# One core, attention and two MLP blocks: batch 2 alone through the first MLP, side-by-side heads, early conversions shared with GpSimd

## The chip, the cores and the metric

One core of a Trainium2 chip runs the whole program. The metric is the device time of one execution in microseconds; a smaller number is better. The kernel before has a median of 1398.46 us over 3 runs (1396.95 to 1399.26).

## The reference, cut to what matters

Four batches of 448 tokens and 768 channels pass through attention with capped scores, a layer norm with an MLP, and a mixer block with a token MLP and a second MLP. All of it is float32.

```python
# attention: batch 4, 12 heads, 448 tokens, 64 channels a head
scores = cap * np.tanh(np.matmul(q, k.transpose(0, 1, 3, 2)) * scale / cap)
attn = np.exp(scores - np.max(scores, axis=-1, keepdims=True))
attn = attn / (np.sum(attn, axis=-1, keepdims=True) + 1e-09)
x = np.matmul(attn, v)                       # to (4, 448, 768)
# first block
xn = (x - mu) / np.sqrt(var + 1e-06) * g_ln
x = x + np.maximum(xn @ w_ch1, 0.0) @ w_ch2  # 768 -> 3072 -> 768
# second block
h = np.maximum(x.transpose(0, 2, 1) @ w_tok1, 0.0) @ w_tok2   # 448 -> 256 -> 448
u = x + h.transpose(0, 2, 1)
out = u + np.maximum(u @ w_ch1, 0.0) @ w_ch2  # 768 -> 1536 -> 768
```

## The kernel before, in words

**Products.** Each float32 factor of the MLPs is split into a high and a low value in a rounded format that TensorE takes fast (`fp32r`), and a product is made of three matmuls: high by high, low by high, high by low (`PASSES`). Every matmul streams the 448 tokens of one batch.

**MLP.** The hidden channels are cut into groups of 512: six groups for the first MLP (0 to 5), three for the second (6 to 8). A group is four tiles of the first weight matrix (18 matmuls a batch each, line 587) and six tiles of the second (12 matmuls a batch each, line 608), so 144 matmuls for one batch. The results are taken out of PSUM by ScalarE and VectorE (lines 592, 593) and added to `x` by VectorE (line 612). `mlp(plan)` walks a list of (group, batches): with two batches ("a pair") one loaded weight tile serves both, with one batch ("alone") it serves one. Weight tiles lie in a ring of three (`split0` to `split2`).

**Weights.** When a tile is needed for the first time, `piece` loads the raw float32 words and converts them: two steps on ScalarE (lines 276, 277), three on VectorE (278, 279 and the addition in 280), a copy that gives the high value on either engine, and a subtraction that gives the low value on VectorE (recorded at line 172, the helper `low`). There are 14 pieces a group, 8 of 384 columns and 6 of 512. The result is also written to a buffer in HBM (`kept`, line 300), and every later use loads it from there (line 296).

**Heads.** Batches 0 and 1 do attention at the start of the program, in plain float32. The heads of batches 2 and 3 are woven into the MLPs of batches 0 and 1: one head at a time, 8 score matmuls (line 366), tanh and exp on ScalarE, a maximum on VectorE (line 374), high and low parts of the exponentials (`eh`, `el`), and the products with the values. These come in two forms. In the plain form (batch 2 before) high and low values go through 11 matmuls in three shapes (lines 411, 413, 414), and a column of ones gives the row sums (read by VectorE at line 433). With a batch in `BESIDE` (batch 3 before) high and low values stand side by side in one 128 column weight, 7 matmuls do (line 408), VectorE sums the exponentials itself (line 421) and the two halves are added (line 430). Lines 341 and 342 load a head's queries and keys (480 KB) and values (192 KB); a late head has one buffer for each, so each load waits for the head before. Two subtractions of a late head may go to GpSimd (also recorded at line 172).

**Order.** Every operation is a step with a key. `Program.emit` plays the steps through a list of costs and puts on each engine the ready step with the smallest key, so the order in the program is fixed when it is built. The numbers `T_...`, `PACE...`, `N...` set the keys. All loads of the late stages, all writes of `kept` and of the output stand in one queue, SyncE's (SP), and are issued in order.

**Sequence of the main stages.** Group 0 of batch 0 alone; groups 1 to 5 of the pair (0, 1); tokens of batch 0 woven with group 0 of batch 1; tokens of batch 1 woven with group 6 of batch 0; groups 7 and 8 of the pair; group 6 of batch 1 alone; then batch 2 alone for `n1` groups, the pair (2, 3) for the other groups of the first MLP, tokens of batch 2 woven with batch 3's `n1` groups alone, tokens of batch 3 woven with groups 6 and 7 of batch 2, the pair for group 8, and groups 6 and 7 of batch 3 alone.

Of the kernel before, what the change touches and what calls it, by code (L numbers as in the profile page):

```python
# [15 lines left out]
ALU = mybir.AluOpType  # L16
# [42 lines left out]

URGENT, SCORES, PREPARE, LOAD = 1000.0, 19.31, 4.58, 24.58  # L60

BESIDE = (3,)

N0, N1, N20, N2 = 1, 3, 1, 2
T_LN0, T_LN1 = 7.69, -20.0
T_AHEAD, N_AHEAD, AHEAD_PACE = 14.0, 1, 5.0
T_ALONE, STRETCH0, T_PAIR, STRETCH1 = 85.0, 1.3, 165.0, 1.14
T_ATT2, PACE2, T_ATT3, PACE3 = 171.18, 25.0, 500.0, 40.0
LEAD, RAW_AHEAD, EVACUATE, TOKENS_AHEAD = 6.3, 9.57, -7.49, 17.25


# [15 lines left out]
class Program:  # L87
# [11 lines left out]
    def add(self, engine, cols, run, reads=(), writes=(), early=0.0):  # L99

        names = [(name.strip("*+"), "*" in name, "+" in name) for name in engine.split("/")]
        costs = {e: self.FIXED[e] + self.RATE[e] * cols * (0.5 if half else 1.0) for e, half, _ in names}
        step = Step(costs, run, (self.key - early, len(self.steps)))
        step.port = {e for e, _, port in names if port}
        before = set()
        for b in [p for b in reads for p in b.parts]:
            before.add(b.writer)
            b.readers.append(step)  # L110
        for b in [p for b in writes for p in b.parts]:
            before.add(b.writer)
            before.update(b.readers)
            b.writer, b.readers = step, []
        before -= {None, step}
        for s in before:
            s.users.append(step)
        step.waits = len(before)
        self.steps.append(step)
# [32 lines left out]
def block_kernel(ctx: ExitStack, tc: tile.TileContext, qkv, cap, gln, w1, w2, wt1, wt2, con, out):  # L152
    nc = tc.nc
    mm, act, dve = nc.tensor.matmul, nc.scalar.activation, nc.vector
    engine_of = {"dve": nc.vector, "pool": nc.gpsimd}
    prog = Program()
    add = prog.add
# [13 lines left out]
    def low(eng, out, whole, high):  # L171
        eng.tensor_tensor(out, whole, high.bitcast(F32), op=ALU.subtract)  # L172

    def copy(e, out, a):
        if e == "act":
            act(out, a, AF.Copy)  # L176
        else:
            dve.tensor_copy(out, a)
# [20 lines left out]
    BIG = [[Box(t[:, e]) for e in range(NCC)] for t in big_t]  # L199
# [6 lines left out]
    def area(n):  # L206
        ends.append(ends[-1] + n)
        return area_t[:, ends[-2]:ends[-1]]
# [6 lines left out]
    two = [Box(area(S)), Box(area(S))]  # L215
# [17 lines left out]
    def ring(of):  # L233
        while True:
            yield from of
# [28 lines left out]


    raws, wholes = ring(RAW), ring(WHOLE)
    kept = {}

    def piece(src, m, target, to):

        r, w = next(raws), next(wholes)
        f = w.at.bitcast(I32)[:, :m]
        words = r.at.bitcast(I32)[:, :2 * m].rearrange("p (n two) -> p n two", two=2)
        lo, hi = words[:, :, 0], words[:, :, 1]
        add("dma", m, lambda: nc.sync.dma_start(out=r.at.bitcast(I64)[:, :m], in_=src), (), [r], early=RAW_AHEAD)
        add("act", m, lambda: act(f.bitcast(F32), hi.bitcast(F32), AF.Copy, scale=2.0 ** -112), [r], [w])  # L276
        add("act", m, lambda: act(lo, lo.bitcast(U32), AF.Copy, scale=2.0 ** -29), (), [r])  # L277
        add("dve+", m // 2, lambda: dve.tensor_scalar(f, f, 3, None, op0=ALU.logical_shift_left), (), [w])  # L278
        add("dve+", m, lambda: dve.scalar_tensor_tensor(f, hi, -(1 << 31), f, op0=ALU.bitwise_and, op1=ALU.bitwise_or), [r], [w])  # L279
        add("dve+", m, lambda: dve.tensor_tensor(f, f, lo, op=ALU.add), [r], [w])  # L280
        g = f.bitcast(F32)
        add("act/dve*+", m, lambda e: copy(e, target[:, 0], g), [w], to)
        add("dve+", m, lambda e: low(engine_of[e], target[:, 1], g, target[:, 0]), [w], to)

    def load(no, w, row, cols):

# [42 lines left out]
    def attention(b, start, pace):  # L329
        x = x_t[b]  # L330
        early, beside = b < 2, b in BESIDE
        rs, rm = rs_t[b % 2], rm_t[b % 2]
# [146 lines left out]
    centred = two + own  # L479
# [54 lines left out]
    def normalise(b):  # L534
        rstd = RSTD[0]
        eng = LN_ENGINES[b]
        for e in range(NCC):
            o, g = centred[e], BIG[b % 2][e]
            if b >= 2:
                subtract(b, e, o)  # L540
            add("dve+", S, lambda o=o, e=e: dve.scalar_tensor_tensor(
                o.at, o.at, gl[:, e:e + 1], rstd.at, op0=ALU.mult, op1=ALU.mult), [rstd, GL], [o])
            add("act", S, lambda g=g, o=o: act(g.at[:, 0], o.at, AF.Copy), [o], [g])  # L543
            add(eng, S, lambda eng, g=g, o=o: low(engine_of[eng], g.at[:, 1], o.at, g.at[:, 0]), [o], [g])
# [13 lines left out]
    def prepare(g):  # L558

        nonlocal n_tile  # L560
        rows = [(w1, g * G + i, C) for i in range(G)] + [(w2, g * NCC + e, G * P) for e in range(NCC)]
        for w, row, cols in rows:
            load(n_tile, w, row, cols)
            n_tile += 1
            prog.key += AHEAD_PACE
# [148 lines left out]
    with tc.manual_schedule():  # L714
        setup()
        prog.key = T_AHEAD
        for g in range(N_AHEAD):
            prepare(g)
        prog.key = 0.0
        attention(0, 0.0, 3.97)  # L720
        prog.key += T_LN0
        layer_norm(0)
        normalise(0)
        head_banks = side_banks = ring(BANKS[:2])
        attention(1, 60.01, 6.39)
        prog.key += T_LN1
        layer_norm(1)
        normalise(1)
        head_banks = side_banks = ring(BANKS[:1])

        main_banks = ring(BANKS[2:])
        n0, n1, n2 = N0, N1, N2
        prog.key, stretch = T_ALONE, STRETCH0
        weave(mlp(groups((0,), 0, n0)))
        main_banks = chain(BANKS[2:], ring(BANKS[1:]))
        attention(2, T_ATT2, PACE2)
        layer_norm(2)
        attention(3, T_ATT3, PACE3)
        prog.key, stretch = T_PAIR, STRETCH1
        weave(mlp(groups((0, 1), n0, NG1 - n0)))  # L740
        weave(tokens(0, HIDDEN[2]), mlp(groups((1,), 0, n0)), ahead=TOKENS_AHEAD)
        weave(tokens(1, HIDDEN[2]), mlp(groups((0,), NG1, N20)), ahead=TOKENS_AHEAD)
        weave(mlp(groups((0, 1), NG1 + N20, NG2 - N20), (0,)))
        weave(mlp(groups((1,), NG1, N20), (1,)))
        normalise(2)
        stretch = 1.0
        weave(mlp(groups((2,), 0, n1)))
        layer_norm(3)
        normalise(3)
        weave(mlp(groups((2, 3), n1, NG1 - n1)))  # L750
        weave(tokens(2, HIDDEN[2]), mlp(groups((3,), 0, n1)), ahead=TOKENS_AHEAD)
        weave(tokens(3, HIDDEN[2]), mlp(groups((2,), NG1, n2)), ahead=TOKENS_AHEAD)
        weave(mlp(groups((2, 3), NG1 + n2, NG2 - n2), (2,)))
        weave(mlp(groups((3,), NG1, n2), (3,)))
        prog.emit()
# [41 lines left out]
```

## Time and profile before

| | |
|---|---|
| median of 3 runs | 1398.46 us (1396.95 to 1399.26) |
| the profiled execution | 1399.07 us |
| its span, first to last instruction | 1397.3 us |
| TensorE busy (matmuls) | 1370.9 us, 98% |
| TensorE weight loads | 1178.4 us, 84% |
| VectorE busy | 887.7 us, 64% |
| ScalarE busy | 612.0 us, 44% |
| GpSimd busy | 63.2 us, 5% |
| moved by DMA | 262.16 MB, mean 188 GB/s |

The busy shares are means over stages of different kinds: VectorE is nearly full in the first 800 us, where weights are converted and heads run, and nearly idle after that. Matmuls overlap in the records (one is shown as some 365 ns long while the next starts some 203 ns after it), so the time that a matmul costs is read from start to start.

### The profile page before, as it was taken

How to read it: one execution, taken by the hardware profiler on the slowest of the kernel's cores; microseconds unless marked ns; L12 is line 12 of the kernel's file. 1: busy time of each engine (PE TensorE's matmuls, PEld its weight loads, DVE VectorE, ACT ScalarE, POOL GpSimd, SP SyncE). 2: the span in 40 equal slices, each digit the busy share in tenths (PEclk: the TensorE clock that was granted, in tenths of full speed). 3: DMA queues.
4: the chain of work that ended last, by engine and by line, in shares of the span. 5: the costliest groups of instructions: out<-in, count | busy, mean ns of one | idle time of the engine just before them, and what ended most of it. 6: DMA issues, size and time to landing. Idle time of an engine off the chain costs nothing.

```text
span 1397.3 us, 17773 instructions
## 1 busy us (share of the span) xinstructions
PE 1370.9 (98%) x6512; PEld 1178.4 (84%) x6512; DVE 887.7 (64%) x1602; ACT 612.0 (44%) x995; POOL 63.2 (5%) x52
## 2 busy tenths in 40 slices
PE   8999989999999999999999999999999999999998
PEld 3335578889898999988999999999999999999997
DVE  5999698988898899999989973212122232232221
ACT  7986567675657656776656421010100111111000
POOL 0000002010011001100010000000000000000000
PEclk9999999999999999999999999999999999999999
DMA  8885447667675756467565576643232456554366
GB/s 264 275 268 161 142 123 244 226 203 227 196 229 191 240 177 223 156 218 235 192 202 195 178 232 200 208 149 128 84 122 93 148 166 189 186 168 151 124 197 194
DMA packets 135671, 262.16 MB, mean 188 GB/s; under 512 B 10144, under 2 KB 72864, under 8 KB 135584
## 3 DMA queue, kind: packets, MB, share of 16 engines
q1 hardware_dynamic: 135008, 260.74, 57.9%
q8 instruction: 51, 0.84, 0.2%
q10 hardware_dynamic: 576, 0.29, 0.1%
q14 instruction: 36, 0.29, 0.1%
HBM read 198.86 MB, written 62.13 MB: 187 GB/s over the span
## 4 chain that ended last, share of the span: by engine, by line
PE 89%; DVE 6%; ACT 3%; DMA 1%; issue 1%; SPq 0%; ACTq 0%; DVEq 0%
PE bank L587 37%; PE bank L608 37%; PE sc L366 3%; PE bank L384 3%; PE bank L682 2%; PE bank L663 2%; PE bank L408 1%; PE sc L363 1%; DVE m L374 1%; ACT x L369 1%; PE bank L414 1%; PE bank L413 1%; PE bank L466 1%; ACT x L370 1%; PE bank L639 1%
## 5 line engine op out<-in xcount | busy, mean ns | idle before, releaser
L608 PE MATMUL bank<-h,split 128*128 128x448 f32 x2592 | 547.9, 367 | 3.4 <-DVE x L612 2.9
L587 PE MATMUL bank<-big,split 128*128 128x448 f32 x2592 | 548.1, 368 | 3.0 <-ACT big L543 2.0
L587 PEld LDWEIGHTS bank<-big,split 128*128 128x128 f32 x2592 | 485.9, 188 | 48.2 <-ACT big L543 3.3
L608 PEld LDWEIGHTS bank<-h,split 128*128 128x128 f32 x2592 | 484.9, 188 | 46.7 <-DVE x L612 3.6
L592 ACT ACTIVATE h<-bank 128x448 fp32r<-128x448 f32 x144 | 78.3, 544 | 398.1 <-PE bank L587 397.6
L612 DVE TENSOR_TENSOR x<-x,bank 128x448 f32<-128x448 f32 x216 | 133.4, 619 | 186.1 <-PE bank L608 184.0
L593 DVE SCALAR_TENSOR_TENSOR h<-bank,h 128x448 fp32r<-128x448 f32 x144 | 89.3, 621 | 183.9 <-ACT h L592 183.3
L276 ACT ACTIVATE whole<-raw 128x384 f32<-128x384 f32 (+2 forms) x130 | 77.6, 600 | 45.4 <-DVE split L172 42.0
L280 DVE CUSTOM_DVE_ANT_0 whole<-raw,whole 128x768 uint16<-128x768 uint16 (+2 forms) x130 | 85.6, 659 | 0.6
L172 DVE TENSOR_TENSOR split<-whole,split 128x384 fp32r<-128x384 f32 (+1 forms) x126 | 79.2, 632 | 4.3 <-ACT split L176 3.6
L279 DVE SCALAR_TENSOR_TENSOR whole<-raw,whole 128x384 int32<-128x384 int32 (+2 forms) x130 | 81.3, 627 | 0.2
L277 ACT ACTIVATE raw<-raw 128x384 int32<-128x384 uint32 (+2 forms) x130 | 77.6, 600 | 0.0
L176 ACT ACTIVATE split<-whole 128x384 fp32r<-128x384 f32 (+1 forms) x85 | 47.9, 564 | 43.6 <-PE bank L608 19.7
L172 POOL TENSOR_TENSOR ks<-area,ks 64x512 fp32r<-64x512 f32 x23 | 31.7, 1377 | 675.5 <-ACT ks L347 675.5
L374 DVE TRANSPOSE_TENSOR_REDUCE m<-x 128x28 f32<-128x896 f32 x48 | 52.5, 1101 | 8.2 <-ACT x L370 7.7
L278 DVE TENSOR_SCALAR whole<-whole 128x384 int32<-128x384 int32 (+2 forms) x130 | 53.7, 416 | 2.3 <-ACT whole L276 1.9
L374 DVE TRANSPOSE_TENSOR_REDUCE m<-area 128x28 f32<-128x896 f32 x48 | 52.9, 1102 | 0.8 <-ACT area L370 0.8
L369 ACT ACTIVATE area<-sc,tsc 128x896 f32<-128x896 f32 x48 | 48.2, 1005 | 11.1 <-DVE el L400 6.3
L370 ACT ACTIVATE area<-area,cap_t 128x896 f32<-128x896 f32 x48 | 49.9, 1040 | 0.6
L369 ACT ACTIVATE x<-sc,tsc 128x896 f32<-128x896 f32 x48 | 46.7, 996 | 6.9 <-DVE tsc L252 4.3
L394 ACT ACTIVATE eh<-area 128x896 fp32r<-128x896 f32 x48 | 45.4, 946 | 9.4 <-PE bank L408 3.5
L370 ACT ACTIVATE x<-x,cap_t 128x896 f32<-128x896 f32 x48 | 49.0, 1037 | 0.3
(117 smaller groups left out, 1116.0 us busy)
## 6 DMA issues: line engine op xcount, KB each, us to landing
split<-kept SPq DMA_DIRECT2D x136, 384.0 KB, 4.1
split<-kept SPq DMA_DIRECT2D x102, 512.0 KB, 3.7
raw<-in_w SPq DMA_DIRECT2D x72, 384.0 KB, 3.5
kept<-split SPq DMA_DIRECT2D x72, 384.0 KB, 3.6
raw<-in_w SPq DMA_DIRECT2D x54, 512.0 KB, 4.0
kept<-split SPq DMA_DIRECT2D x54, 512.0 KB, 3.3
area<-in_qkv SPq DMA_DIRECT2D x38, 480.0 KB, 4.1
area<-in_qkv SPq DMA_DIRECT2D x35, 192.0 KB, 3.3
```

The costliest lines, as they stand in the source:

```text
L172: eng.tensor_tensor(out, whole, high.bitcast(F32), op=ALU.subtract)
L276: add("act", m, lambda: act(f.bitcast(F32), hi.bitcast(F32), AF.Copy, scale=2.0 ** -112), [r], [w])
L279: add("dve+", m, lambda: dve.scalar_tensor_tensor(f, hi, -(1 << 31), f, op0=ALU.bitwise_and, op1=ALU.bitwise_or), [r], [w])
L280: add("dve+", m, lambda: dve.tensor_tensor(f, f, lo, op=ALU.add), [r], [w])
L369: add("act", 2 * S, lambda e=e, sc=sc: act(e, sc.at[:, :, :S], AF.Tanh, scale=tsc), [sc], eb)
L370: add("act", 2 * S, lambda e=e: act(e, e, AF.Exp, scale=cap_t), (), eb)
L374: add("dve", 2 * S, lambda half=half, e=e: dve.tensor_reduce(m.at[:, half].rearrange("p c j -> p (c j)"), e.rearrange("p c (j i) -> p (c j ...
L587: mm(ph.at[:, :S], w[:, wi, cc * P:(cc + 1) * P], src[cc].at[:, xi], start=(cc, n) == (0, 0), stop=(cc, n) == (NCC - 1, 2))
L592: add("act", S, lambda ht=ht, ph=ph: act(ht.at[:, 0], ph.at[:, :S], AF.Relu), [ph], [ht], early=EVACUATE)
L593: add("dve", S, lambda ht=ht, ph=ph: dve.scalar_tensor_tensor(ht.at[:, 1], ph.at[:, :S], 0.0, ht.at[:, 0].bitcast(F32), op0=ALU.max, op1=A ...
L608: mm(py.at[:, :S], w[:, wi, i * P:(i + 1) * P], h[i].at[:, hi], start=(i, n) == (0, 0), stop=(i, n) == (G - 1, 2))
L612: add("dve", S, lambda x=x, py=py: dve.tensor_tensor(x.at, x.at, py.at[:, :S], op=ALU.add), [py], [x], early=EVACUATE)
```

## The change

`BESIDE` takes batch 2 in, so both late batches use the side-by-side form. `N1` goes from 3 to 6: batch 2 does all six groups of the first MLP alone, no group is done by the pair (2, 3), and batch 3 does six groups alone. The late heads get other start keys and paces. In the group that is prepared ahead, at the start of the program, the integer addition (line 280) and the subtraction for the low value go to GpSimd. `normalise` for batches 2 and 3 uses two buffers in turn instead of six, so that it no longer shares the buffers of the late heads' exponentials.

```diff
-BESIDE = (3,)
+BESIDE = (2, 3)
-N0, N1, N20, N2 = 1, 3, 1, 2
+N0, N1, N20, N2 = 1, 6, 1, 2
-T_ATT2, PACE2, T_ATT3, PACE3 = 171.18, 25.0, 500.0, 40.0
+T_ATT2, PACE2, T_ATT3, PACE3 = 230.0, 35.0, 650.0, 25.0
-    kept = {}
+    kept, ahead = {}, False
@@ piece
-        add("dve+", m, lambda: dve.tensor_tensor(f, f, lo, op=ALU.add), [r], [w])
+        add("pool+" if ahead else "dve+", m, lambda e: engine_of[e].tensor_tensor(f, f, lo, op=ALU.add), [r], [w])
-        add("dve+", m, lambda e: low(engine_of[e], target[:, 1], g, target[:, 0]), [w], to)
+        add("pool+" if ahead else "dve+", m, lambda e: low(engine_of[e], target[:, 1], g, target[:, 0]), [w], to)
@@ normalise
-            o, g = centred[e], BIG[b % 2][e]
+            o, g = centred[e] if b < 2 else two[e % 2], BIG[b % 2][e]
@@ block_kernel
         prog.key = T_AHEAD
+        ahead = True
         for g in range(N_AHEAD):
             prepare(g)
+        ahead = False
```

On TensorE, this is the first head of batch 2 before, the first half of its products with the values among the MLP of the pair (0, 1):

```order
L587 MATMUL bank_112<-big_84,split_77 128x448 x12
L411 MATMUL bank_111<-eh_98,vs_97 96x448
L413 MATMUL bank_111<-eh_98,vs_97 64x448
L414 MATMUL bank_111<-el_99,vs_97 96x448
L411 MATMUL bank_111<-eh_98,vs_97 96x448
L413 MATMUL bank_111<-eh_98,vs_97 64x448
L414 MATMUL bank_111<-el_99,vs_97 96x448
L587 MATMUL bank_112<-big_84,split_77 128x448 x6
```

The same half head in the changed program:

```order
L587 MATMUL bank_114<-big_85,split_79 128x448 x12
L408 MATMUL bank_111<-eh_98,vs_97 128x448
L408 MATMUL bank_111<-el_99,vs_97 128x448
L408 MATMUL bank_111<-eh_98,vs_97 128x448
L408 MATMUL bank_111<-el_99,vs_97 128x448
L587 MATMUL bank_114<-big_85,split_79 128x448 x6
```

Six matmuls became four, and the half head stands some tiles later in the MLP. On VectorE, the first piece of the group prepared ahead stands so before (`whole` holds the words in work, `split` the result, `m` and `rs` belong to heads):

```order
L278 TENSOR_SCALAR whole_75<-whole_75 128x384
L279 SCALAR_TENSOR_TENSOR whole_75<-raw_72,whole_75 128x384
L280 ISA whole_75<-raw_72,whole_75 128x768
L374 TENSOR_REDUCE m_100<-x_82 128x28
L433 TENSOR_REDUCE rs_103<-bank_112 32x14
L172 TENSOR_TENSOR split_77<-whole_75,split_77 128x384
L278 TENSOR_SCALAR whole_76<-whole_76 128x384
```

and GpSimd does in the changed program, with the additions and subtractions gone from VectorE's row:

```order
L280 TENSOR_TENSOR whole_75<-whole_75,raw_72 128x384
L172 TENSOR_TENSOR split_77<-whole_75,split_77 128x384
L280 TENSOR_TENSOR whole_76<-whole_76,raw_73 128x384
L172 TENSOR_TENSOR split_77<-whole_76,split_77 128x384
L280 TENSOR_TENSOR whole_75<-whole_75,raw_74 128x384
```

In all 28 instructions move so, for 14 pieces. On SP's queue, where group 6 of batch 1 alone loads its tiles from `kept`, heads of batch 3 now load between them; before, these rows were the `kept` loads one after the other:

```order
L296 DMA split_79<-kept_27_0_219 128x2x384
L296 DMA split_79<-kept_27_384_220 128x2x384
L342 DMA area<-in_qkv 128x384
L296 DMA split_77<-kept_36_0_221 128x2x512
L296 DMA split_78<-kept_37_0_222 128x2x512
L341 DMA area<-in_qkv 128x960
L296 DMA split_79<-kept_38_0_223 128x2x512
```

After the last raw weight load of the program the queue held two loads of values before; it now holds six loads of values and four of queries and keys.

## Rows read from the trace of the kernel before

**Rows 1.** The chain that ended last, share of the span by engine (the page, 4).

```profile
PE 89%; DVE 6%; ACT 3%; DMA 1%; issue 1%; SPq 0%; ACTq 0%; DVEq 0%
```

**Rows 2.** Busy time of each engine in stretches of the span (the first row names columns).

```profile
core 0: us, PE busy (x) PEld busy (x) DVE busy (x) ACT busy (x) POOL busy (x), PEclk, DMA share, GB/s
205.00:550.00 345.00, 345.00 (x1685) 308.51 (x1684) 309.57 (x563) 225.94 (x375) 39.51 (x28) 1.00 0.66 214
550.00:600.00 50.00, 50.00 (x262) 46.60 (x261) 47.85 (x81) 40.11 (x66) 7.85 (x6) 1.00 0.57 188
600.00:650.00 50.00, 45.55 (x229) 41.02 (x228) 46.17 (x89) 32.75 (x63) 4.96 (x4) 0.97 0.71 233
```

**Rows 3.** Timeline of TensorE, one head of batch 2: start us, duration us, instruction.

```profile
275.32 0.36 PE L411 MATMUL bank<-eh,vs 128*96 128x448 f32 x1
...
276.55 0.99 PE L366 MATMUL sc<-qs,ks 128*128 128x448 f32 x4
...
281.09 0.36 PE L411 MATMUL bank<-eh,vs 128*96 128x448 f32 x1
...
282.41 0.97 PE L366 MATMUL sc<-qs,ks 128*128 128x448 f32 x4
```

**Rows 4.** Timeline of TensorE, a second and a first half head of batch 3.

```profile
709.74 0.36 PE L408 MATMUL bank<-eh,vs 128*128 128x448 f32 x1
...
710.35 6.35 PE L608 MATMUL bank<-h,split 128*128 128x448 f32 x30
...
718.61 0.37 PE L408 MATMUL bank<-eh,vs 128*128 128x448 f32 x1
...
719.43 8.67 PE L608 MATMUL bank<-h,split 128*128 128x448 f32 x42
```

**Rows 5.** Groups by line and shape, whole span: count, busy us, mean ns, idle before.

```profile
L172 POOL TENSOR_TENSOR qs<-area,qs 128x448 fp32r<-128x448 f32 x23 | 30.9, 1342 | 8.3 <-DVE qs L178 4.6 <-ACT qs L176 2.1
...
L421 DVE TRANSPOSE_TENSOR_REDUCE n<-area 128x28 f32<-128x896 f32 x24 | 26.3, 1097 | 0.0
...
L433 DVE TRANSPOSE_TENSOR_REDUCE rs<-bank 32x14 f32<-32x448 f32 x36 | 23.3, 648 | 17.0 <-ACT x L436 9.2 <-PE bank L414 3.8 <-PE sc L363 2.1
...
L430 DVE TENSOR_TENSOR x<-bank,area 64x448 f32<-64x448 f32 x12 | 7.3, 612 | 1.3 <-ACT area L429 1.1
```

**Rows 6.** The two conversion steps that move, all pieces (the page, 5).

```profile
L280 DVE CUSTOM_DVE_ANT_0 whole<-raw,whole 128x768 uint16<-128x768 uint16 (+2 forms) x130 | 85.6, 659 | 0.6
L172 DVE TENSOR_TENSOR split<-whole,split 128x384 fp32r<-128x384 f32 (+1 forms) x126 | 79.2, 632 | 4.3 <-ACT split L176 3.6
```

**Rows 7.** Busy time of each engine at the start, in the columns of Rows 2.

```profile
50.00:100.00 50.00, 47.01 (x145) 19.51 (x145) 48.02 (x84) 46.27 (x63) 0.00 (x0) 0.93 0.82 270
```

**Rows 8.** Chain that ended last within 55 to 95 us, by line.

```profile
by line: DVE m L374 20.5%; issue 10.1%; DVE split L172 8.4%; DVE rs L433 8.2%; PE sc L363 7.8%; PE bank L466 7.1%; DVE whole L279 6.0%; ACT x L369 4.8%; ACT x L370 4.2%; DVE whole L278 2.9%; DVE x L469 2.9%; DVE whole L280 2.7%; DVE area L4
```

**Rows 9.** Timeline of all engines, tokens of batch 1 (the bracket: idle before).

```profile
600.71 1.27 POOL L172 TENSOR_TENSOR ks<-area,ks 64x512 fp32r<-64x512 f32 x1 [18.48 <-ACT ks L347]
600.87 1.52 DVE L280 CUSTOM_DVE_ANT_0 whole<-raw,whole 128x768 uint16<-128x768 uint16 x1
...
604.12 1.77 PE L682 MATMUL bank<-t,h 128*128 128x448 f32 x5 [2.08 <-DVE h L669]
```

**Rows 10.** Pieces of the chain that ended last: start us, us, line, matmuls.

```profile
843.20 14.59 PE bank L608 x72
...
945.34 29.18 PE bank L608 x144
...
1348.29 14.88 PE bank L608 x72
```

**Rows 11.** Waits of SP's queue, 205 to 830 us: us in total, times, longest.

```profile
SPq L341 <- POOL qs L172: 35.7, 18, 4.0
...
SPq L342 <- DVE vs L172: 22.8, 14, 3.6
```

**Rows 12.** Loads of line 296, 830 to 915 us, batch 2 alone: time to landing.

```profile
DMA to landing us min/median/max: 3.5/3.9/6.2
```

## Prediction

> **What bounds the kernel now.** I read the chain of work that ended last first: 89% of the span is TensorE [rows 1], so a change pays what it takes off TensorE's stream or off a gap in it. Then the stretches [rows 2]: from 205 to 550 us TensorE is busy for all 345.00 us while VectorE is busy for 309.57, and it stays whole from 550 to 600 us with VectorE at 47.85 of 50. Only 600 to 650 us has a hole, 45.55 of 50, with a mean granted clock of 0.97, so some 3 us lie at the lower of the two levels (1.2 instead of 2.4 GHz) behind the idle. The start is different: between 50 and 100 us VectorE has 48.02 and ScalarE 46.27 of 50 [rows 7], and the chain there runs mostly over VectorE [rows 8]. So I cost the change on TensorE from 205 us on, on VectorE and ScalarE before.
>
> **Heads of batch 2 side by side.** In the plain form the first half head of the products takes from 275.32 to 276.55 us, 1.23 us for six matmuls, and the second from 281.09 to 282.41, 1.32 us for five [rows 3]: 2.55 us a head. In the side-by-side form a second half takes 709.74 to 710.35, 0.61 us, and a first half 718.61 to 719.43, 0.82 us [rows 4]: 1.43 us. The score matmuls are the same. 12 heads x 1.12 us = 13.4 us less on an engine that has no gap in these stretches.
>
> The rows give the plain form 0.20 to 0.26 us a matmul, the narrow ones of the second half the most [rows 3]. The Trainium skill ("TensorE: Matmul & The Clock Gate", "Back-to-back issue gap") gives a lone matmul its streamed columns over 2.4 GHz plus 2.5 ns, which would be 189 ns for 448 columns whatever the weight's width, and by it the four matmuls less save an estimated 9.1 us. I go by the rows.
>
> What it adds on VectorE: two sums of 1.10 us and an addition of 0.61, less the row-sum reduction of 0.65 [rows 5], so 2.2 us a head and 26 us in all. The 35.4 us that VectorE has free between 205 and 550 us [rows 2] cover most of it, the heads now start later and further apart, and 550 to 600 us shows a VectorE at 96% that costs TensorE nothing. I take a loss of 0.5 us. The bounds are 0 and 6 us, the upper one the 4.45 us hole of 600 to 650 us with the 1.5 us that its slow clock cost, once more [rows 2].
>
> **Batch 2 alone for six groups.** The matmuls are the same number; three groups, 432 matmuls for each of two batches, go from pair to alone, and some 18 MB more (three groups of 8 x 384 + 6 x 512 KB) is loaded from `kept`. Alone, 72 matmuls took 14.59 us, in a pair 144 took 29.18: 202.6 ns each both ways [rows 10]. So the move itself costs nothing, as long as loads hide: a tile of 12 matmuls lasts 2.43 us, a load may take the time of two (4.86 us) and lands in 3.9 us (median) [rows 12]. But TensorE has a second pace that no wait explains: near the end 72 matmuls took 14.88 us, 206.7 ns each [rows 10]. Batch 3's three added groups stand in the woven late part, where I expect that pace: 432 x 4.1 ns = 1.8 us. Bounds: 0, and 5.2 us with all of batch 2's six groups in it as well (864 matmuls more).
>
> **Head loads among the lone groups.** Batch 3's heads now run up to the first group of batch 2, and the order shows ten of their loads (six of 192 KB, four of 480) between the `kept` loads of the groups alone. That is 3.1 MB, or 11.7 us at the 270 GB/s of the early stage [rows 7], where a tile's load has only about 1 us to spare. Half of a lone group (18 matmuls a tile) gives loads much more room than the other half, so I charge 2 us; bounds 0 and, if no transfer hides, 11.7.
>
> **The early conversions.** VectorE loses 14 x (0.659 + 0.632) = 18.1 us [rows 6]. GpSimd takes 1342 ns for 448 columns [rows 5], so 1.15 us for 384 and 1.53 for 512, 36.8 us for the 28 steps, if its integer addition runs like its subtraction. What speaks against it: with GpSimd at work from 600.71 us on, line 280 on VectorE took 1.52 us [rows 9] against a mean of 0.66 [rows 6]. So a VectorE step with two SBUF inputs waits for GpSimd, and 36.8 us of GpSimd can eat most of the 18.1. What is free of that is the maxima of line 374, the first entry of the chain there [rows 8]. And ScalarE, with 3.7 us idle in 50 [rows 7], is next in line. I take 2 us of gain; bounds 6 us of gain (ScalarE's idle and as much again ahead of it) and 8 us of loss (18.1 us saved, some 26 of the 36.8 come back as waits).
>
> **The tokens of batch 1.** The hole at 600 to 650 us begins where a head's two GpSimd steps hold up VectorE, whose evacuation (line 669) comes late: TensorE idle for 2.08 us [rows 9]. In the new order no head is prepared there, but layer norm 2 moves in, about as much VectorE work at once. Gain 1.5 us; bounds 6 us of gain (the whole hole) and 2 of loss (a second wait like that one).
>
> **Two buffers in `normalise`.** Its cover is the last pair group and batch 1's lone group, over 50 us; nothing.
>
> Sum: -13.4 + 0.5 + 1.8 + 2.0 - 2.0 - 1.5 = -12.6 us. The profiled execution took 1399.07 us, 1.8 more than its span; it lies 0.6 above the median of 1398.46. Against the median that makes 1385.9, so **1386 us**.
>
> **Rivals.**
> - *SP's queue takes the gain back* (slower). A head's load waits in the queue for the buffer of the head before, and every `kept` load behind it waits too: 35.7 us in 18 waits for queries and keys and 22.8 in 14 for values before [rows 11], 2.0 and 1.6 us each. Behind pairs these were hidden. Six and four such waits in the lone groups are 17.7 us; if none hides, 1386 - 2 + 17.7 = 1402 us. It decides from about 1 us a wait on, the room that a load has there. For it: the mean waits are over that. Against it: only some of the ten stand before tiles that are needed at once.
> - *GpSimd holds up VectorE at the start.* 8 us of loss instead of 2 of gain: 1396 us. Rows 9 speaks for it, the many port-free maxima against it. The Trainium skill ("GPSIMD Engine Reference", "Performance versus the Vector engine" and "Key points") calls GpSimd the wrong place for elementwise work and says it shares VectorE's SBUF interfaces where that has two SBUF inputs; the trace agrees, 1.34 us for 448 columns [rows 5] against a mean of 0.63 for like steps on VectorE [rows 6].
> - *VectorE becomes the bound of the pair stage.* 26 us more into 35.4 free; two holes like that of 600 to 650 us [rows 2] cost 12 us: 1398 us. Against it: 550 to 600 us.
> - *The change does not do what it says:* batch 2's shorter heads only turn into waits of TensorE for the same evacuations. Without the 13.4 us: 1399 us. Against it: the stretch has no such wait now.
> - *All the small terms turn out well:* early gain 6 us, the hole gone: 1386 - 4 - 4.5 = 1377.5 us.
>
> **How the numbers follow.** Chances: the forecast 0.64 (its own range 1380 to 1392), small terms well 0.12, GpSimd at the start 0.08, VectorE bound 0.05, nothing gained 0.04, SP's queue 0.07. A difference of 0.2% (2.8 us) is about what a measurement of this kernel can tell from no change. Faster: 0.64 + 0.12 + 0.08 + 0.02 = 0.86; within 0.2%, the rest of VectorE and nothing gained: 0.07; slower: 0.07. The range of 1377 to 1396 us leaves out the last three cases and a little at the lower end.
>
> **What would show it.** Right: line 408 for 24 heads and no line 411; TensorE whole from 205 to 600 us with VectorE near 94%; 72 matmuls in 14.6 to 14.9 us in batch 2's groups alone, without gaps; the first pair matmuls a few us earlier; a smaller hole near the tokens of batch 1. Wrong: TensorE waiting for `split<-kept` where batch 1's group 6 and batch 2's group 0 run alone; steps of lines 278 and 279 twice as long in the first 100 us; waits for line 612 or 593 between 205 and 550 us.

## The result and the profile after

The changed kernel takes 1378.23 us (median of 4 runs, 1377.02 to 1379.4) beside 1397.50 us of the kernel before on the same chip: ratio 0.9863, 95% interval 0.985 to 0.9877, so some 19 us less. One execution of an earlier group of runs took 4738.71 us, with the MLP's matmuls a median of 660 ns apart and a granted clock recorded as 1.00; it is left out (the others of that group took 1377.30 to 1379.83 us), and the rows of "after" come from the run called `changed_again`, the same kernel at its usual pace.

| | before | after |
|---|---|---|
| profiled execution, us | 1399.07 | 1377.28 |
| its span, us | 1397.3 | 1375.5 |
| mean granted clock | 0.995 | 0.997 |

The page of the kernel after, part 4: the chain that ended last, by engine.

```profile
PE 92%; ACT 4%; DVE 3%; DMA 1%; issue 1%; ACTq 0%
```

TensorE's share rose from 89% [rows 1] to 92%, VectorE's fell from 6% to 3%. The next rows are the stretches of [rows 2] and [rows 7], in the same columns.

```profile
205.00:550.00 345.00, 345.00 (x1710) 318.38 (x1709) 317.08 (x574) 220.67 (x368) 32.57 (x25) 1.00 0.67 218
550.00:600.00 50.00, 49.84 (x263) 45.44 (x262) 47.30 (x101) 33.15 (x65) 0.00 (x0) 1.00 0.64 209
600.00:650.00 50.00, 50.00 (x254) 45.99 (x253) 48.07 (x95) 36.74 (x67) 2.70 (x2) 1.00 0.72 236
50.00:100.00 50.00, 46.08 (x143) 18.44 (x141) 43.76 (x70) 46.50 (x64) 18.41 (x14) 0.93 0.80 263
```

TensorE is still whole from 205 to 550 us, with VectorE at 317.08 us (92%) where it was 309.57. The hole of 600 to 650 us is gone: 50.00 instead of 45.55 us busy, granted clock 1.00 instead of 0.97. At the start VectorE fell from 48.02 to 43.76 us and GpSimd works beside it. A head of batch 2 on TensorE's timeline (start us, duration us) answers to [rows 3] and [rows 4]:

```profile
281.44 0.36 PE L408 MATMUL bank<-eh,vs 128*128 128x448 f32 x1
...
282.27 2.63 PE L587 MATMUL bank<-big,split 128*128 128x448 f32 x12
284.74 0.99 PE L366 MATMUL sc<-qs,ks 128*128 128x448 f32 x4
...
286.81 0.37 PE L408 MATMUL bank<-eh,vs 128*128 128x448 f32 x1
...
287.42 5.03 PE L608 MATMUL bank<-h,split 128*128 128x448 f32 x24
```

Its halves take 281.44 to 282.27 and 286.81 to 287.42: 0.83 + 0.61 = 1.44 us, where the plain form took 2.55. By the starts of the matmuls the 24 half heads of batch 2 took 30.4 us before and take 17.2 us now, 13.2 us less. In TensorE's list of waits from 205 to 830 us no row is left.

### The profile page after: what moved, and what is told of

Same layout as the page of the kernel before. It is cut to its first block, busy times and chain, and to the rows that moved or that the text cites. A ratio compares the mean times of both kernels' runs of the same rounds, so it can differ in the third digit from the quotient of the medians.

```text
span 4736.9 us, 17816 instructions
## 1 busy us (share of the span) xinstructions
PE 4727.3 (100%) x6464; PEld 2684.3 (57%) x6464; DVE 897.4 (19%) x1612; ACT 624.5 (13%) x1006; POOL 88.9 (2%) x79
## 4 chain that ended last, share of the span: by engine, by line
PE 100%; DMA 0%; ACT 0%; DVE 0%; issue 0%
PE bank L587 39%; PE bank L608 39%; PE bank L384 6%; PE sc L363 3%; PE sc L366 3%; PE bank L408 3%; PE bank L663 2%; PE bank L682 2%; PE bank L639 1%; PE bank L466 1%; PE bank L531 0%; PE bank L495 0%; PE bank L511 0%; DMA area<-in_qkv 0%; PE bank L445 0%; PE bank L444 0%
## 5 line engine op out<-in xcount | busy, mean ns | idle before, releaser
L587 PE MATMUL bank<-big,split 128*128 128x448 f32 x2592 | 1898.3, 994 | 1.1 <-ACT big L543 1.1
L608 PE MATMUL bank<-h,split 128*128 128x448 f32 x2592 | 1895.9, 995 | 0.0
L587 PEld LDWEIGHTS bank<-big,split 128*128 128x128 f32 x2592 | 1109.8, 429 | 749.3 <-issue 739.4
L608 PEld LDWEIGHTS bank<-h,split 128*128 128x128 f32 x2592 | 1109.5, 428 | 744.9 <-issue 741.6
L366 PE MATMUL sc<-qs,ks 128*128 128x448 f32 x192 | 151.5, 993 | 0.0
L384 PE MATMUL bank<-x,area 128*96 128x448 f32 (+1 forms) x88 | 129.4, 1666 | 0.0
L363 PE MATMUL sc<-area 64*128 64x448 f32 x112 | 112.0, 1696 | 4.8 <-DMA area<-in_qkv 4.8
L384 PE MATMUL bank<-x,x 128*96 128x448 f32 (+1 forms) x76 | 112.5, 1675 | 0.0
L682 PE MATMUL bank<-t,h 128*128 128x448 f32 x144 | 108.0, 993 | 0.0
L663 PE MATMUL bank<-big,t 128*128 128x384 f32 x136 | 89.7, 899 | 0.0
```

The costliest lines, as they stand in the source:

```text
L363: mm(sc.at[:, i, :S], k[rows, c * P:(c + 1) * P], q[rows], start=True, stop=True)
L366: mm(sc.at[:, i, :S], ks.at[:, c * P:(c + 1) * P], qs.at[:, j], start=j == 0, stop=j == 1)
L384: mm(po.at[:DV, :S], v.at[:n, c], E[c // 2][0][:n, c % 2], start=c == 0, stop=c == 3)
L587: mm(ph.at[:, :S], w[:, wi, cc * P:(cc + 1) * P], src[cc].at[:, xi], start=(cc, n) == (0, 0), stop=(cc, n) == (NCC - 1, 2))
L608: mm(py.at[:, :S], w[:, wi, i * P:(i + 1) * P], h[i].at[:, hi], start=(i, n) == (0, 0), stop=(i, n) == (G - 1, 2))
L663: mm(pj.at[:, :CC], t1[:, wi, sc * DT + j * P:sc * DT + (j + 1) * P], cols(xs[sc])[:, xi], start=(sc, wi, xi) == (0, 0, 0), stop=(sc, wi) ...
```

## The experiments

Each kernel was timed beside the kernel before on the same chip; the kernel before has medians of 1397.50 to 1397.89 us there. A ratio is to that median, with its 95% interval. What "205 to 550" and the like say is the span's time.

**1. The change again.** No edit; it gives the profile above and the reference for what follows.

> The changed kernel once more, unaltered, for a profile at the usual TensorE pace. Measured so far 1377.3 to 1379.8 us, some 20 us under the kernel before, against a forecast of 12.6. Theory A (the heads' matmuls carry the gain, and one of the small terms was sized too low): TensorE spends 13.4 us less on the products with the values, and the other 6 to 7 us show as fewer or shorter gaps of TensorE, either before 205 us or at the tokens of batch 1 (a hole of 4.45 us busy time before). Rival B (the pace decides): no gap is smaller, and the rest comes from stretches at 202.6 instead of 206.7 ns a matmul; 6 us would need some 1500 matmuls at the quicker pace.

Measured: 1378.23 us. As Theory A said, the heads' products are 13.2 us shorter and the hole at the tokens of batch 1 is gone (both shown above). Rival B is wrong: the mean from start to start of the MLP's matmuls is 203.93 ns before and 204.06 ns after.

**2. Side by side alone.** The kernel before with one line changed.

```diff
-BESIDE = (3,)
+BESIDE = (2, 3)
```

> The kernel before with batch 2's heads side by side and nothing else; starts, paces and N1 as before. Theory A: -13.4 us of TensorE work, with up to 6 us of it given back where VectorE has 2.2 us more a head at the old, denser pace: 1385 to 1391 us. Rival (VectorE becomes the bound without the later, slower heads): waits for lines 612 or 593 between 205 and 550 us, and 1392 us or more.

Measured: 1397.05 us, ratio 0.9997 (0.9988 to 1.0006). The rival is right: the edit that carries my largest term gives nothing by itself. Its stretch of 205 to 550 us, in the columns of [rows 2]:

```profile
205.00:550.00 345.00, 336.74 (x1645) 306.49 (x1645) 324.95 (x595) 226.06 (x379) 35.56 (x25) 1.00 0.66 215
```

and TensorE's waits from 205 to 830 us (us in total, times, longest):

```profile
PE bank L608 <- DVE x L612: 3.8, 5, 1.1
PE sc L366 <- ACT area L369: 3.8, 4, 2.4
PE bank L608 <- ACT raw L277: 2.1, 1, 2.1
```

VectorE is at 324.95 us (94%), and TensorE, whole before, stands still for 8.26 us here. It waits for its banks to be emptied (line 612) and for ScalarE, which waits for VectorE in turn. TensorE was relieved; VectorE, which feeds it, had no room for the 2.2 us that each head adds. The idle is the larger part of the loss, not all of it: the profiled execution is 2.2 us shorter than that of the kernel before, so 11 of the heads' 13.2 us are lost, against 8.3 us more of idle in the whole span and an estimated 1.4 us of clock (a mean of 0.994 instead of 0.995).

**3. GpSimd alone.** The kernel before with only the two steps of the prepared group on GpSimd (the two `"pool+" if ahead else "dve+"` lines and the flag around `prepare`).

> The kernel before with the two GpSimd steps in the group prepared ahead and nothing else. Forecast of the prediction: -2 us, within +8 and -6. Theory A1 (the start holds what the forecast missed): -6 to -9 us, and the first matmul of line 587 comes that much earlier. Rival (GpSimd holds VectorE up and the missing gain lies elsewhere): 0 to +8 us, with lines 278 and 279 twice as long in the first 100 us.

Measured: 1395.75 us, ratio 0.9984 (0.9975 to 0.9993): 1.75 us less, about what the prediction charged. Neither the 6 to 9 us of Theory A1 nor the rival's loss is there.

**4. The change with plain heads.**

```diff
-BESIDE = (2, 3)
+BESIDE = (3,)
```

> The changed kernel with batch 2's heads back in the plain form. Theory A: the 13.4 us come back, 1391 to 1393 us from 1378.5, less what VectorE gains by 26 us of work less. Rival (the heads' saving is hidden by something else, and the gain comes from the new order): under 1385 us.

Measured: 1392.02 us, ratio 0.9967 (0.9954 to 0.998). In the changed kernel the heads of batch 2 are worth 13.8 us; alone they were worth nothing. All the rest of the change gives 5.5 us, 1.75 of it GpSimd's. Two stretches of this kernel (columns of [rows 2]) show where most of the others lie:

```profile
550.00:600.00 50.00, 48.98 (x253) 44.80 (x252) 45.24 (x82) 35.87 (x64) 7.92 (x6) 1.00 0.53 176
600.00:650.00 50.00, 49.30 (x255) 45.22 (x254) 47.23 (x93) 35.60 (x64) 2.45 (x2) 1.00 0.71 232
```

The idle there is 1.7 us instead of 4.45, and the clock is whole, so the hole at the tokens of batch 1 does not need the new form of the heads to close. Experiment 10 has the new times without GpSimd's steps, the two buffers and the six groups, and there too 550 to 660 us is busy for 109.23 of 110 us at a clock of 1.00.

**5. Batch 2's heads at their old times.** What in the change gives side by side its room? First the times: the changed kernel with batch 2's old start and pace.

```diff
-T_ATT2, PACE2, T_ATT3, PACE3 = 230.0, 35.0, 650.0, 25.0
+T_ATT2, PACE2, T_ATT3, PACE3 = 171.18, 25.0, 650.0, 25.0
```

> The changed kernel with batch 2's heads where they stood before (one every 25 from 171.18 instead of one every 35 from 230); all else as changed. Theory A (side by side pays only where VectorE has room, and the later, slower heads make it): VectorE's share of 205 to 550 us rises from 92% to about 94%, TensorE waits there again at L608, L366 and L682 for 5 us or more, and the time is 1384 to 1394 us. Rival B (six groups of batch 2 alone make the gain, since they leave the later stages room, and where its heads stand matters little): 1377 to 1381 us, no more than 2 us of waits between 205 and 550.

Measured: 1393.99 us, ratio 0.9972 (0.9961 to 0.9984), 15.8 us of the gain lost by two numbers. The stretch is that of experiment 2 again:

```profile
205.00:550.00 345.00, 338.08 (x1642) 306.64 (x1642) 325.30 (x591) 219.71 (x369) 36.74 (x26) 0.99 0.66 215
```

VectorE 94%, TensorE idle for 6.92 us, as Theory A said. That is less than half of the loss. The profiled executions lie 17.0 us apart, and the mean granted clock of the whole span is 0.992 here and 0.997 in experiment 1, an estimated 7 us.

**6. Three groups of batch 2 alone.**

```diff
-N0, N1, N20, N2 = 1, 6, 1, 2
+N0, N1, N20, N2 = 1, 3, 1, 2
```

> The changed kernel with three groups of batch 2 alone before the late pair, as before, instead of six; heads of both batches keep their new times. Theory A (the six groups are what gives batch 3's later heads the time they need): its heads, started at 650 with one every 25, are not done when the late pair starts near 830 us, TensorE waits there for its tokens or its heads stand close together, and the time is 1385 to 1410 us. Rival B (the heads fit in three groups too, and six only cost the slower pace of TensorE in lone groups): 1374 to 1378 us, with no wait over 1 us near 830.

Measured: 1376.45 us, ratio 0.9843 (0.983 to 0.9856), no wait listed from 205 to 830 us. Theory A is wrong here. The part that names the change, six groups of batch 2 alone, is not needed: the heads of batch 3 fit in three, as Rival B said, and the time is no longer than with six (the intervals of the two ratios overlap).

**7. The change without GpSimd.** The line `ahead = True` is left out.

> The changed kernel with the two early steps back on VectorE; all else as changed. Theory A (GpSimd's gain is early and adds to the rest, as it did alone: 1.75 us): 1379.5 to 1381 us, with the first MLP tile's matmul 1 to 2 us later. Rival B (in the changed kernel the early gain is lost in a later wait, or is larger since the stage behind it starts sooner): under 1378.8, or over 1382 us.

Measured: 1381.61 us, ratio 0.9882 (0.9868 to 0.9896). The medians differ by 3.4 us from experiment 1, above Theory A's band and under the 1382 us of Rival B; the two intervals of the ratio overlap, and the two runs are of different chips. So GpSimd's part in the changed kernel is known no better than some 2 to 3.4 us. First matmul of an MLP: 2.3 us later than in experiment 1.

**8. The sums of a late head twice.** The two line-421 sums of a head are done a second time to the same place, which leaves the values as they were.

```diff
-                    add("dve", 2 * S, lambda half=half, e=e: dve.tensor_reduce(
+                    for again in range(2):
+                        add("dve", 2 * S, lambda half=half, e=e: dve.tensor_reduce(
```

> The changed kernel with each of the two sums of a late batch's head (L421, 1.10 us each) done a second time to the same place: 2.2 us more of VectorE for each of 16 heads, 8 of them between 205 and 550 us, where VectorE's busy time rises from 317 to about 333 of 345 us (97%). Theory A (past about 94% TensorE waits for VectorE): 5 to 18 us of waits in 205 to 550 us at L608, L366 and L682, and 1383 to 1398 us. Rival B (28 us of VectorE's time are idle there, so 18 more are hidden): under 1380 us.

Measured: 1393.85 us, ratio 0.9974 (0.9965 to 0.9984). (The late heads are 24, not the 16 of the expectation.) The size is that of Theory A, the place is not:

```profile
205.00:550.00 345.00, 343.66 (x1702) 317.22 (x1701) 317.48 (x558) 210.94 (x352) 29.50 (x22) 1.00 0.66 217
550.00:860.00 310.00, 302.83 (x1491) 274.11 (x1490) 287.35 (x509) 186.30 (x309) 33.08 (x22) 0.99 0.62 204
```

In the first stretch VectorE is no busier than in the changed kernel (317.08), though it does 20 us more of sums there (48.5 us of line 421 beside 28.6): other work of VectorE slipped behind. TensorE loses 1.3 us there and 7.2 us in the next stretch, where the changed kernel lost 0.23. So VectorE's idle 28 us are no store to draw on; what it takes over is paid a stage later. The mean granted clock, 0.994 instead of 0.997, adds an estimated 4 us. Since nothing on TensorE was touched, this run shows that load on VectorE alone can eat the gain.

**9. The two edits together, batch 2 only.** The kernel before with side by side for batch 2 and its new times.

```diff
-BESIDE = (3,)
+BESIDE = (2, 3)
...
-T_ATT2, PACE2, T_ATT3, PACE3 = 171.18, 25.0, 500.0, 40.0
+T_ATT2, PACE2, T_ATT3, PACE3 = 230.0, 35.0, 500.0, 40.0
```

> The kernel before with two edits: batch 2's heads side by side, and one every 35 from 230 instead of one every 25 from 171.18. Three groups of batch 2 alone, batch 3's heads from 500 with one every 40, and all conversions on VectorE, as before. Theory A (the later heads alone let side by side pay): 13.4 us for the heads and about 4 for the hole at 600 to 650 us, so 1379 to 1384 us, with under 2 us of waits between 205 and 550 us. Rival B (batch 3's later heads or the six groups are needed as well): VectorE waits move to 550 to 830 us, where both batches' heads then stand, and the time is 1386 to 1397 us.

Measured: 1395.78 us, ratio 0.9985 (0.9976 to 0.9994). Theory A holds up to 550 us (TensorE 344.93 of 345 us), then the loss is where Rival B put it:

```profile
550.00:600.00 50.00, 49.50 (x254) 44.16 (x252) 47.99 (x94) 34.39 (x67) 0.00 (x0) 1.00 0.58 194
600.00:650.00 50.00, 44.90 (x216) 39.81 (x217) 48.36 (x98) 35.79 (x62) 3.98 (x3) 0.97 0.51 168
650.00:700.00 50.00, 46.66 (x212) 41.37 (x212) 42.52 (x75) 32.20 (x51) 6.44 (x6) 0.93 0.58 189
```

Batch 3's heads still start at 500, before batch 2's later ones are through. VectorE has 47.99 and 48.36 of 50 us, and TensorE stands still for 8.4 us between 600 and 700 us, with a mean granted clock of 0.97 and 0.93 (part of it at the lower of the two levels, 1.2 GHz).

**10. The times of both batches.** As experiment 9, with batch 3's new times too.

```diff
-T_ATT2, PACE2, T_ATT3, PACE3 = 171.18, 25.0, 500.0, 40.0
+T_ATT2, PACE2, T_ATT3, PACE3 = 230.0, 35.0, 650.0, 25.0
```

> The kernel before with two edits: batch 2's heads side by side, and the times of both batches' heads as in the change (one every 35 from 230, one every 25 from 650, each with 12 heads). Three groups of batch 2 alone and all conversions on VectorE, as before. Theory A (the loss of the run before this lay where the heads of both batches overlapped, from 550 to 830 us, and the times of both batches are what lets side by side pay): no wait list over 2 us from 205 to 830 us, and 1378 to 1382 us, that is the changed kernel with three groups and some 2 to 4 us for GpSimd's part. Rival B (the early conversions on GpSimd, or the six groups, carry part of it): 1385 to 1397 us.

Measured: 1399.16 us, ratio 1.0006 (0.9998 to 1.0015). This is outside both bands: Theory A is wrong by 17 us, and Rival B's 1397 is passed too. Three stretches:

```profile
205.00:550.00 345.00, 345.00 (x1715) 319.31 (x1714) 313.81 (x579) 218.78 (x363) 32.88 (x26) 1.00 0.68 222
550.00:660.00 110.00, 109.23 (x555) 98.89 (x554) 105.24 (x210) 76.29 (x140) 5.52 (x4) 1.00 0.64 210
660.00:830.00 170.00, 158.97 (x750) 142.32 (x749) 149.14 (x253) 98.60 (x148) 17.23 (x14) 0.96 0.56 186
```

Up to 660 us the theory holds; the losses of experiments 2 and 9 are gone. Then 11.03 us of idle and a granted clock of 0.96 appear in a stretch that had none before. The kernel of experiment 6 has this instead:

```profile
660.00:830.00 170.00, 170.00 (x841) 157.21 (x840) 149.78 (x257) 96.94 (x148) 18.12 (x13) 1.00 0.63 210
```

The idle and an estimated 6.8 us for the clock (0.04 of 170 us) make 17.8 us in this one stretch. Line by line, this kernel differs from that of experiment 6 (1376.45 us) in two edits only, the early conversions, which end in the first 100 us, and the buffers of `normalise`. The timelines point to the buffers. First TensorE in this kernel:

```profile
823.51 3.08 PE L587 MATMUL bank<-big,split 128*128 128x448 f32 x6 [2.77 <-ACT big L543]
...
831.44 0.68 PE L587 MATMUL bank<-big,split 128*128 128x448 f32 x2 [1.02 <-ACT big L543]
```

and VectorE, where lines 484 and 541 are `normalise` of batch 2, lines 421 and 430 the sums and the last addition of batch 3's heads, and `area` the tile that holds both the buffers of `normalise` and the exponentials of the late heads:

```profile
820.15 1.06 DVE L374 TRANSPOSE_TENSOR_REDUCE m<-area 128x28 f32<-128x896 f32 x1
821.14 1.11 DVE L484 TENSOR_TENSOR area<-x,mean 128x448 f32<-128x448 f32 x2
822.17 1.27 DVE L541 SCALAR_TENSOR_TENSOR area<-area,gl,rstd 128x448 f32<-128x448 f32 x2
...
825.72 1.10 DVE L421 TRANSPOSE_TENSOR_REDUCE n<-area 128x28 f32<-128x896 f32 x1
...
828.36 0.63 DVE L430 TENSOR_TENSOR x<-bank,area 64x448 f32<-64x448 f32 x1 [1.11 <-ACT area L429]
829.02 1.16 DVE L484 TENSOR_TENSOR area<-x,mean 128x448 f32<-128x448 f32 x2
830.10 1.28 DVE L541 SCALAR_TENSOR_TENSOR area<-area,gl,rstd 128x448 f32<-128x448 f32 x2
```

In the kernel of experiment 6 steps of `normalise` stand here:

```profile
726.85 0.68 DVE L541 SCALAR_TENSOR_TENSOR area<-area,gl,rstd 128x448 f32<-128x448 f32 x1
...
744.77 0.68 DVE L541 SCALAR_TENSOR_TENSOR area<-area,gl,rstd 128x448 f32<-128x448 f32 x1
...
747.21 0.68 DVE L541 SCALAR_TENSOR_TENSOR area<-area,gl,rstd 128x448 f32<-128x448 f32 x1
```

With two buffers that the heads don't use, `normalise` of batch 2 is through at 748 us, some 40 us before batch 2's first product at 791 us, and batch 3's last heads lie between the products of batch 2's lone groups. With six buffers, four of them shared with those heads, its last four steps can only run once the heads are nearly through, at 822 and 830 us: the program lists `attention(3)` ahead of `normalise(2)`, and `add` makes a step that writes a buffer wait for every earlier step that reads it. The last two follow 0.03 us behind the last head's addition (line 430). Batch 2's products begin at 799 us and get on by 36 matmuls up to 830 us; the last heads stand there without them, and TensorE waits for both. In the kernel before nothing of this was seen, since batch 3's last scores started at 773 us, `normalise` ended at 805 us, and batch 2's first product stood at 827 us.

**11. An odd matmul in the late groups.** Near the end of the program TensorE runs lone groups at 206.7 ns a matmul, earlier at 202.6, and no wait explains it [rows 10]. This kernel is the changed one with a matmul of 64 columns ahead of the first product of six late groups.

```diff
                         def product(part=part, w=w, src=src, ph=ph, jog=jog):
+                            if jog:
+                                mm(ph.at[:, S:512], w[:, 0, :P], src[0].at[:, 0, :512 - S], start=True, stop=True)
                             for cc in (2 * part, 2 * part + 1):
```

> The changed kernel with one extra matmul of 64 columns (into 64 unused columns of the PSUM bank) ahead of the first product of six late groups, between 1057 and 1375 us, where lone groups ran at 206.7 ns a matmul and not at 202.6 ns as earlier. It changes nothing of the output. Theory C (the pace is a state of TensorE that an odd matmul can change): pieces of 72 matmuls after the extra one take 14.59 us instead of 14.88 us in at least some of the groups, up to 5 us in all, and the time is 1373 to 1377 us. Rival D (the pace hangs on something else, as where the data lie or what the DMA does then): the pieces keep 14.88 us, and the time is 1378 to 1380 us.

Measured: 1373.79 us, ratio 0.9831 (0.9816 to 0.9846), and this interval does not reach that of experiment 1. The chain that ended last in the changed kernel without the extra matmul (start us, us, line, matmuls):

```profile
1071.36 14.88 PE bank L608 x72
1086.24 14.88 PE bank L587 x72
1101.12 14.88 PE bank L608 x72
...
1251.84 29.76 PE bank L587 x144
```

and with it (line 589 is the extra matmul, 592 and 613 are the lines 587 and 608 of above):

```profile
1070.60 14.88 PE bank L613 x72
1085.48 0.03 PE bank L589
1085.51 14.66 PE bank L592 x72
1100.17 14.59 PE bank L613 x72
...
1279.17 29.19 PE bank L613 x144
```

The piece right ahead of the first extra matmul still takes 14.88 us, the long ones behind it 14.59 to 14.67 per 72 matmuls. The mean from start to start of all products falls from 204.06 to 203.27 ns, 4.1 us for 5184 matmuls, which is the whole gain. Theory C's forecast came true; what in TensorE the odd matmul changes is not shown.

**12. Three groups and the odd matmul.** The edits of experiments 6 and 11 together, the extra matmul ahead of seven groups.

> The changed kernel with three groups of batch 2 alone instead of six, and the extra matmul of 64 columns ahead of seven late groups. Theory C (the gains of both add, as each keeps matmuls at 202.6 ns in another stretch): the slow stretches left by three groups are about 26 us from 1146 and 115 us from 1251, which at 2% less give 2.8 us, less 7 extra matmuls, so 1373 to 1375 us. Rival D (the pace of a stretch is not set by the extra matmul): 1376 to 1379 us.

Measured: 1375.07 us, ratio 0.9835 (0.9822 to 0.9848). It lies between Theory C's band and Rival D's, and its interval overlaps those of experiments 6 and 11, so the two gains do not visibly add. By its median the fastest kernel of the study is that of experiment 11, which beats the changed one by about 4 us. Near the end of its chain stands a load:

```profile
1352.35 4.88 PE bank L613 x24
1357.23 0.02 issue
1357.25 4.86 DMA split<-kept
```

The last two tiles wait for their load, 4.86 us on the chain that ended last, as they did before the change (5.35 us).

## Why the prediction came out as it did

The direction was right, and 1378.2 us lies in the range, near its lower end: the gain is 19.3 us where the sum gave 12.6. The largest term was right in mechanism and size. That the change keeps it is in part luck: the two conditions for it, the heads' times and the buffers, were not costed, and the same reasoning would have given much the same sum for the kernels of experiments 5 and 10, which take 1394 and 1399 us. Term by term:

- **Heads side by side, -13.4 us.** The mechanism and the size are right in the changed kernel: 1.44 us a head, 13.2 us for all of them, and 13.8 us between it and its twin with plain heads (experiment 4). What the text left open is the condition. The Trainium skill ("TensorE: Matmul & The Clock Gate", "Back-to-back issue gap") would have made it an estimated 9.1 us; the measurement sides with the rows. With nothing else changed the rival "the change does not do what it says" was the truth, 1397.05 against its 1399 us (experiment 2).
- **VectorE's extra work, +0.5 us.** Right in the changed kernel, where 205 to 550 us is whole at 317.08 us. But the argument, that 35.4 us are free for 26 of work, was not sound. Experiments 2, 5 and 8 show it: with 94% on VectorE in this stretch, or with more of the same work at 92%, the loss is 13 to 16 us, 7 to 8.5 of it as idle time of TensorE. The rival "VectorE becomes the bound of the pair stage" (1398 us) is what experiment 2 shows. It is the spacing of the heads that made the term small, which I named in half a sentence and did not cost. With it the stretch takes up 7.5 us more of VectorE work, not 26, since two heads of batch 3 moved out of it. The "VectorE near 94%" that I named as a sign of being right is the share at which experiments 2 and 5 lose.
- **Two buffers in `normalise`, "nothing".** This is the weakest step. As a cost it was right: `normalise` is through long before batch 2's first product. What it missed is what the edit buys. I named as its cover the work ahead of that product, 50 us of it, and did not ask who holds the six buffers at that time. With the late times of the change it is batch 3's heads. The kernel of experiment 10 differs from that of 6 by this edit and GpSimd's, and is 22.7 us slower; less 1.75 to 3.4 for GpSimd (experiments 3 and 7) the buffers are worth 19 to 21 us. It differs from that of 7 by this edit and the number of groups, and is 17.6 us slower, with 0 to 1.8 for the groups 17.6 to 19.4. Both ways it is about 19 us, as much as the whole change gains. Taking the buffers alone out of the changed kernel was not tried, so this price rests on the two differences and on the timelines of experiment 10.
- **The hole at the tokens of batch 1, -1.5 us.** Right in sign, too small: its 4.45 us of idle are gone and the clock there is whole, so about 4.3 us and some 1.5 of clock, near the bound of 6 that I gave. The reason given holds as well: GpSimd has no step from 541 to 626 us, so no head is prepared ahead of these tokens. Experiment 4 shows most of it without the new heads. With some 4.3 us more than charged this is the largest part of the 6.7 us that I missed; the head loads (2) and the pace (1.2) are the rest.
- **Head loads among lone groups, +2 us.** Mis-sized: TensorE has no wait for `split<-kept` between 205 and 830 us. SP's queue waited as before, 38.1 us in 18 waits at line 341 where [rows 11] has 35.7, so the rival that costs this at 17.7 us was wrong in its step from the queue's wait to TensorE's.
- **Slow pace, +1.8 us.** The place is right: batch 3's lone groups run at 206.7 ns. From 1057 us on the mean from start to start went from 205.11 to 206.04 ns, an estimated 1.3 us. All of the products together went only from 203.93 to 204.06 ns, so some 0.6 us for 5184 matmuls, since between 550 and 830 us the mean fell from 204.08 to 203.22 ns, which I had not looked for.
- **The early conversions, -2 us.** Right: 1.75 us alone (experiment 3). The 28 steps took 32.6 us of GpSimd, not 36.8, and the hold-up of VectorE is there but small:

```profile
L280 POOL TENSOR_TENSOR whole<-whole,raw 128x512 int32<-128x512 int32 x6 | 8.2, 1374 | 8.9 <-ACT whole L276 3.2 <-ACT raw L277 3.1 <-ACT x L436 1.9
...
L280 POOL TENSOR_TENSOR whole<-whole,raw 128x384 int32<-128x384 int32 x8 | 8.1, 1013 | 30.0 <-DVE whole L279 17.2 <-ACT x L369 5.6 <-DMA x<-in_qkv 3.0
```

  VectorE's line 279 beside it went from a mean of 545 to 623 ns for 384 columns and from 671 to 820 ns for 512 (groups by line and shape of the first 100 us, before and after), 1.6 us in all; neither is twice as long, the sign of being wrong that I gave. Against the 18.1 us of work taken off VectorE that is little, so the rule that GpSimd shares VectorE's SBUF interfaces (the Trainium skill, "GPSIMD Engine Reference", "Key points") agrees with the trace and does not decide the time.
- **Six groups of batch 2 alone.** Costed at nothing but pace, and so it is: with three groups the time is no longer (experiment 6). It is not where the gain comes from.

So 13.8 of the 19.3 us have one source, the shorter stream on TensorE; the other 5.5 come without it (experiment 4), mostly from the closed hole and GpSimd. Three edits keep the 13.8 us from being given back, each in a stage of its own: batch 2's later heads for 205 to 550 us, batch 3's later heads for 600 to 700, and, as read from the differences above, the two buffers for 790 to 840. Side by side with none of them, with the first, and with the first two takes 1397.1, 1395.8 and 1399.2 us; with all three, three groups alone and GpSimd's steps it takes 1376.5.

## What to carry to other kernels

In this kernel, work taken off the engine that bounds it paid only where the engine that feeds it had room in the same stretch, and idle time counted over a long stretch is no proof of room: look at how close together the moved work stands. When an edit moves a step in time, list what it shares a buffer with at its new time; an edit that seems free on its own may be what the others depend on. Parts of a change are not to be added up: do each one alone and take each one out, and where the two differ, look for the stage that gives the gain back.

## What the runs showed of the hardware

TensorE has two lasting paces for the same stream of 128 x 448 matmuls, 202.6 and 206.7 ns, both at a granted clock recorded as 1.00. One matmul of 64 columns ahead of a group changed the slower into the quicker in long pieces of the late groups (experiment 11: 14.88 us, then 14.59 to 14.67 for 72 matmuls). Why it does was not found.
